# Loading the MLP's weights ahead of the first K block and the output weights behind the last V block, in a decode kernel on one core

## Chip, core and metric

The kernel runs on one core of one Trainium2 chip. The metric is the time of one execution on the device in microseconds (us), lower is better. The kernel before takes 402.87 us (median of 4 runs, 402.78 to 402.98). "The profile" is one execution taken by the hardware profiler; times inside it count from the start of its span.

The engines go by the profile's names: PE is TensorE (PEld its weight loads), DVE is VectorE, ACT is ScalarE, POOL is GpSimd, and SP is SyncE, which here issues the transfers. "Issue" in a chain of waits is time in which an engine waited for nothing that the profile shows. The granted clock is the share of its full clock that PE was allowed. K0, V0 and so on are the blocks of the cache, counted from 0.

## The reference, cut to what matters

One token (x has 1024 numbers) goes through attention with a K and V cache and, beside it, through an MLP.

```python
# A: q = LN(x) @ wq (32 heads of 128); 4 K/V heads of 65536 x 128, 8 queries to each
#    softmax(q k^T / sqrt(128)) v, then @ wo (4096 x 1024)
# B: h  = gelu(LN(xn) @ w1); shift by one or two tokens (S = 1: only zeros are left) @ w2; x1 = xn + that
#    h2 = gelu(LN(x1) @ w3) @ w4;   w1, w2: 1024 x 1024, w3: 1024 x 3584, w4: 3584 x 1024
xn = LN(x)
out = x + A(xn) + x1 + h2
```

Everything is bfloat16. K and V are 134 MB of the 170 MB that are read; the weights are the rest.

## The kernel before

The cache is read as 16 pairs of blocks (4.19 MB of K, 4.19 MB of V each) into two slots of each of two buffers, `Kn` and `Vn`. Each pair is two steps `n`. A step transposes a K half block on DVE into `X` (`Ttr`), multiplies it with q on PE (`QK`), takes maxima, exponentiates on ACT, transposes and multiplies with V (`PV`), and adds into an accumulator on POOL (`FLASH`). When a head is done, its accumulator is normalised and folded into 128 x 8 numbers by `combine`: two products on PE, each with steps on DVE before and after it.

The transfers are all issued in order by SP, and each waits only for its target to be free. The weights pass one after another through a buffer `W`, each issued in the middle of the loop:

```python
        orow = sb("orow", [P, 256], BF)
        W = sb("W", [P, 14336], BF)
        X = sb("X", [P, 2, 8192], BF)
        Kn = sb("Kn", [P, 2, 16384], BF)
        Vn = sb("Vn", [P, 2, 16384], BF)
        # [cut]
        w_seq = [(0, w1_dma, 3, w1_pe), (4, w2_dma, 7, w2_pe),
                 (8, lambda: w3_dma(0), 11, lambda: w3_pe(0)), (12, lambda: w3_dma(1), 15, lambda: w3_pe(1)),
                 (16, lambda: wo_dma(0), 19, lambda: wo_pe(0)), (20, lambda: wo_dma(1), 23, lambda: wo_pe(1))]
        # [cut]
        for n in range(NT):
            h, nb = divmod(n, NSUB)
            QK(n)
            Ttr(n + 1, [0])
            stats1(n)
            if nb == 0 and h > 0:
                combine_1(h - 1)        # the head before, inside the loop
            MB(n); stats2(n); EXP(n)
            Ttr(n + 1, [1])
            if nb == 0 and h > 0:
                combine_2(h - 1)
            PTr(n)
            Ttr(n + 1, [2, 3])
            PV(n); FLASH(n)
            # [cut: products and loads of w_seq, the next K or V block, wo 2 and 3, w4]
        wo_pe(HKV - 2)
        combine_1(HKV - 1)
        combine_2(HKV - 1)
        wo_pe(HKV - 1)
        for i in range(len(w4_parts)):
            w4_pe(i)
```

The combine itself:

```python
        def combine_1(h):
            PE : M0_ps[:, 0:1] = Dmat_f^T @ O_acc[:, 512:513]
            DVE: cb_rL = 1 / M0_ps[:, 0:1];  cb_W = maskT * cb_rL      # 128 x 512
        def combine_2(h):
            PE : M0_ps[:, 128:256] = sum over t of cb_W[t]^T @ O_acc[:, t]   # fp32, 4 products
            DVE: cb_R = M0_ps * maskD;  cb_o = reduce(cb_R);  o_bf[h] = cast(cb_o)
```

(The second block is shortened to its data flow.) Everything goes through one `M0_ps`, one `cb_W` and one `cb_R`.

## Time and profile before

| reading | before | where |
|---|---|---|
| time | 402.87 us | runs |
| bytes read | 169.87 MB, 98.4% of 16 engines' span | queue table |
| K waited for by DVE | 67.4 us in 11 waits | table of waits |
| PE waits for w4 in the tail | 5.0 us in 4 waits | table of waits |
| last w4 piece lands | 398.81 us | chain in order of time |
| final cast starts | 399.50 us | chain in order of time |

The page of the kernel before: its span; the share of time that its 16 DMA engines are busy, in 40 slices, in tenths; its bytes moved; the main queue; and the chain of waits by engine.

```profile
span 401.7 us, 4776 instructions
...
DMA  8999999999999999999999999999999999999994
GB/s 359 424 418 438 445 418 424 460 419 421 436 447 419 429 435 435 422 436 445 420 428 450 426 419 441 441 419 428 434 439 421 447 432 424 426 425 436 437 416 207
...
q1 hardware_dynamic: 6920, 169.87, 98.4%
...
DMA 55%; DVE 24%; PE 16%; issue 2%; ACT 1%; SPq 0%; another core or an unknown queue 0%; POOL 0%; ACTq 0%
...
```

No slice but the first and last is below 90%. (Single slices read up to 460 GB/s because the page counts a packet whole in the slice in which it starts; spread over the time of each packet, no 10 us of this trace exceed 434 GB/s.) The transfers bind; what matters is when the last one lands and what comes after it. The table of waits (engine, line, what it waited for, us in total, times, longest):

```profile
...
DVE X L476 <- DMA Kn<-in_A_k_cache_dram: 67.4, 11, 9.2
...
PE OUT_ps L404 <- DMA Kn<-in_B_w_dram: 5.0, 4, 1.9
...
```

PE waits 5.0 us in all for the four parts of w4. PE's instructions (start, duration, what it is, and in brackets the idle time before it and what ended it):

```profile
...
383.50 0.38 PE L554 MATMUL M_ps<-O_acc,Dmat_f 128*128 128x1 f32 x2 [0.36 <-POOL O_acc L550]
384.67 1.16 PE L564 MATMUL M_ps<-O_acc,cb_W 128*128 128x128 f32 x8 [0.78 <-DVE cb_W L557]
386.92 1.88 PE L404 MATMUL OUT_ps<-W,o_bf 128*1 128x256 bf16 x32 [1.09 <-DVE o_bf L571]
390.37 2.98 PE L404 MATMUL OUT_ps<-Kn,gh_bf 128*1 128x256 bf16 x56 [1.58 <-DMA Kn<-in_B_w_dram]
...
398.85 0.59 PE L404 MATMUL OUT_ps<-Kn,gh_bf 128*1 128x256 bf16 x8 [0.19 <-DMA Kn<-in_B_w_dram]
```

One combine runs from 383.50 to about 386.9, then the last wo product, then each part of w4 as soon as it is there. The end of the chain of waits, in order of time:

```profile
...
374.44 24.37 DMA Kn<-in_B_w_dram
...
399.50 0.42 DVE orow L631
```

### The profile page before, as it was taken

To read this page: it belongs to the slowest core of one execution; us is meant where nothing else is said; L and a number is where in the kernel's file an instruction comes from. 1 tells how busy PE (TensorE), PEld (TensorE's weight loads), DVE (VectorE), ACT (ScalarE), POOL (GpSimd) and SP (SyncE) were. 2 spreads that over 40 slices of the span, in tenths; PEclk is the share of its full clock that TensorE was granted. 3 is DMA by queue.
4 is the path that set the end of the run, shared out by engine and by line. 5 is a ranking of instruction groups with operands and counts; after the bars stand their busy time and mean duration, and the time that the engine had idled before them with its cause. 6 is when DMAs were issued, how large, how long until landed. Compare 5 with 4: busy or idle time off the path is not lost.

```text
span 401.7 us, 4776 instructions
## 1 busy us (share of the span) xinstructions
PE 186.4 (46%) x1859; PEld 78.5 (20%) x1875; DVE 228.4 (57%) x401; ACT 48.9 (12%) x128; POOL 61.8 (15%) x90
## 2 busy tenths in 40 slices
PE   0332325064525745285531965353433654444664
PEld 0211101021103511062110731121111311111132
DVE  0247566277816578255744287576836775788410
ACT  1000111011101011011110011111201111112100
POOL 5000003012211011110310101111110112112110
PEclk9985556556565556555655555656555656565566
DMA  8999999999999999999999999999999999999994
GB/s 359 424 418 438 445 418 424 460 419 421 436 447 419 429 435 435 422 436 445 420 428 450 426 419 441 441 419 428 434 439 421 447 432 424 426 425 436 437 416 207
DMA packets 7087, 170.19 MB, mean 424 GB/s; under 512 B 916, under 2 KB 920, under 8 KB 1048
## 3 DMA queue, kind: packets, MB, share of 16 engines
q1 hardware_dynamic: 6920, 169.87, 98.4%
q8 instruction: 15, 0.25, 0.2%
q14 instruction: 8, 0.07, 0.0%
q10 hardware_dynamic: 144, 0.00, 0.0%
HBM read 169.87 MB, written 0.00 MB: 423 GB/s over the span
## 4 chain that ended last, share of the span: by engine, by line
DMA 55%; DVE 24%; PE 16%; issue 2%; ACT 1%; SPq 0%; another core or an unknown queue 0%; POOL 0%; ACTq 0%
DMA Kn<-in_A_k_cache_dram 44%; DVE X L476 13%; DMA Kn<-in_B_w_dram 6%; DMA Vn<-in_A_wq_dram 5%; PE H_ps L366 4%; PE S_ps L488 3%; DVE pT_f L529 3%; PE OT_ps L536 3%; DVE mrow L495 3%; PE M_ps L366 1%; ACT p_sb L518 1%; PE PT_ps L527 1%; PE M_ps L564 1%; PE OUT_ps L404 1%; DVE Yall L393 1%
## 5 line engine op out<-in xcount | busy, mean ns | idle before, releaser
L476 DVE STREAM_TRANSPOSE X<-Kn 128x1024 f32<-128x1024 f32 x128 | 151.7, 1215 | 67.4 <-DMA Kn<-in_A_k_cache_dram 67.4
L536 PE MATMUL OT_ps<-Vn,pT_f 128*32 128x512 bf16 x512 | 60.7, 627 | 52.4 <-DVE pT_f L529 52.4
L488 PE MATMUL S_ps<-X,Yall 128*32 128x512 bf16 x512 | 59.1, 608 | 16.1 <-DVE X L476 16.1
L501 PE MATMUL MB_ps<-Rm,Lmat 128*128 128x16 bf16 x32 | 6.1, 192 | 90.1 <-DVE Rm L496 90.1
L550 POOL TENSOR_TENSOR O_acc<-O_acc,tmpO 128x513 f32<-128x513 f32 x28 | 32.8, 1172 | 88.6 <-ACT tmpO L544 88.6
L518 ACT ACTIVATE p_sb<-S_ps,brun 128x512 bf16<-128x512 f32 x32 | 22.0, 687 | 192.7 <-DVE brun L516 157.3
L548 POOL TENSOR_SCALAR O_acc<-O_acc,ff 128x513 f32<-128x513 f32 x28 | 19.5, 698 | 153.4 <-ACT ff L523 153.4
L495 DVE TENSOR_REDUCE mrow<-S_ps 128x1 f32<-128x512 f32 x32 | 21.6, 674 | 25.5 <-PE S_ps L488 25.5
L544 ACT ACTIVATE tmpO<-OT_ps 128x512 f32<-128x512 f32 x32 | 19.1, 598 | 108.0 <-PE OT_ps L536 108.0
L488 PEld LDWEIGHTS S_ps<-X,Yall 128*32 128x32 bf16 x512 | 16.6, 126 | 54.7 <-DVE X L476 38.2
L529 DVE STREAM_TRANSPOSE pT_f<-PT_ps 128x512 f32<-128x512 f32 x32 | 22.9, 716 | 6.1 <-PE PT_ps L527 4.2
L536 PEld LDWEIGHTS OT_ps<-Vn,pT_f 128*32 128x32 bf16 x512 | 14.6, 129 | 59.2 <-DVE pT_f L529 42.0
L501 PEld LDWEIGHTS MB_ps<-Rm,Lmat 128*128 128x128 bf16 x32 | 3.3, 102 | 114.9 <-DVE Rm L496 114.9
L527 PE MATMUL PT_ps<-p_sb,permR 128*128 128x512 bf16 x16 | 9.3, 580 | 21.4 <-ACT p_sb L518 21.4
L366 PEld LDWEIGHTS H_ps<-xn_bf,W 128*128 128x128 bf16 x224 | 14.4, 169 | 1.7 <-issue 1.7
L366 PE MATMUL H_ps<-xn_bf,W 128*128 128x1 bf16 x224 | 14.5, 202 | 0.0
L527 PEld LDWEIGHTS PT_ps<-p_sb,permR 128*128 128x128 bf16 x32 | 3.4, 105 | 41.4 <-ACT p_sb L518 41.4
L505 DVE TENSOR_REDUCE Bst<-MB_ps 128x1 f32<-128x16 f32 x32 | 5.6, 174 | 8.3 <-PE MB_ps L501 8.3
L330 PE MATMUL M_ps<-ln_s,ones_f 128*128 128x1 f32 x6 | 1.8, 362 | 17.3 <-DVE ln_s L329 17.3
L546 POOL COPY O_acc<-tmpO 128x513 f32<-128x513 f32 x4 | 2.4, 612 | 47.4 <-ACT tmpO L544 47.4
L404 PE MATMUL OUT_ps<-Kn,gh_bf 128*1 128x256 bf16 x112 | 5.6, 364 | 5.0 <-DMA Kn<-in_B_w_dram 5.0
L631 DVE CAST orow<-OUT_ps 128x256 bf16<-128x256 f32 x1 | 0.4, 425 | 12.7 <-PE OUT_ps L404 12.7
(109 smaller groups left out, 116.6 us busy)
## 6 DMA issues: line engine op xcount, KB each, us to landing
Kn<-in_A_k_cache_dram SPq DMA_DIRECT2D x15, 4096.0 KB, 27.3
Vn<-in_A_v_cache_dram SPq DMA_DIRECT2D x15, 4096.0 KB, 23.3
W<-in_B_w_dram SPq DMA_DIRECT2D x2, 3584.0 KB, 24.9
W<-in_A_wo_dram SPq DMA_DIRECT2D x3, 2048.0 KB, 23.8
Kn<-in_A_wq_dram SPq DMA_DIRECT2D x1, 4096.0 KB, 12.1
Vn<-in_A_wq_dram SPq DMA_DIRECT2D x1, 4096.0 KB, 21.2
W<-in_B_w_dram SPq DMA_DIRECT2D x2, 2048.0 KB, 33.8
Kn<-in_A_k_cache_dram SPq DMA_DIRECT2D x2, 2048.0 KB, 25.3
```

What stands on the lines that cost most here:

```text
L366: fns.append(lambda e, j=j, cx=cx: e.matmul(ps_tile[:, c0 + cx:c0 + cx + 1], lhs_fn(j - j0, cx), rhs_fn(j), start=(j == 0 and cx == 0), st ...
L404: fns.append(lambda e, lhs=lhs, rhs=rhs, jj=jj: e.matmul(OUT_ps[32 * jj:32 * jj + 1, 0:256], lhs, rhs[:, 256 * jj:256 * jj + 256], start=F ...
L476: _op(q_dve, lambda e, ix=ix: e.transpose(out=X32[:, xs, 1024 * ix:1024 * (ix + 1)], in_=Kn32[:, s, 4096 * half + 1024 * ix:4096 * half + ...
L488: fns.append(lambda e, we=we, cm=cm, mv=mv: e.matmul(S_ps[32 * cm:32 * cm + 32, :], Yall[:, h, we, :, :].rearrange("p a g -> p (a g)"), mv ...
L495: _op(q_dve, lambda e: e.reduce_max(mrow[:, m:m + 1], S_ps[:, :], axis=AX.X), reads=[b_S], writes=[b_mrow[m]])
L518: _op(q_act, lambda e: e.activation(p_sb[:, m, :], S_ps[:, :], ACTF.Exp, bias=brun[:, kn:kn + 1], scale=SCALE, accum_out=tmpO[:, m, 512:513]),
L527: _op(q_pe, lambda e: e.matmul(PT_ps[:, :], permR[:, :], p_sb[:, m, :], start=True, stop=True), reads=[b_p[m], b_const], writes=[b_PT])
L529: _op(q_dve, lambda e: e.transpose(out=pT_f[:, :], in_=PT_ps[:, :]), reads=[b_PT], writes=[b_pT])
L536: fns.append(lambda e, q=q, q4=q4: e.matmul(OT_ps[32 * q4:32 * q4 + 32, :], pT_bf[:, q, :, 1], Vn[:, s, 8192 * half + 512 * q:8192 * half ...
L544: _op(q_act, lambda e: e.activation(tmpO[:, m, 0:512], OT_ps[:, :], ACTF.Copy), reads=[b_OT], writes=[b_tmpO[m]], partial=True)
L548: _op(q_pool, lambda e: e.tensor_scalar(out=O_acc[:, :], in0=O_acc[:, :], scalar1=ff[:, m:m + 1], scalar2=0.0, op0=ALU.mult, op1=ALU.add), ...
L550: _op(q_pool, lambda e: e.tensor_tensor(out=O_acc[:, :], in0=O_acc[:, :], in1=tmpO[:, m, :], op=ALU.add), reads=[b_tmpO[m]], writes=[b_Oacc])
```

## The change

The intent: get rid of the buffer `W` and of the bursts of MLP work inside the loop, by loading w1, w2 and w3 at the very start into buffers that K, V and X do not need yet, and wo and w4 at the end into buffers that they no longer need. The combines leave the loop as well; each head gets its own accumulator. MLP products keep the activation as the stationary operand and stream the weights ("row form": 128 matmuls of 256 or 448 columns in place of 352 of one column). The residual is added in the final cast instead of by 64 small matmuls.

The diff, cut to its core (the cut parts: a routine for rolling PE's program into a loop, which is not called; the helpers of the row form; renamed buffers; equal bodies for all steps):

```diff
-        W = sb("W", [P, 14336], BF)
         X = sb("X", [P, 2, 8192], BF)
+        load_rows(Kn[:, 0, 0:8192], [b_K[0][0]], "w1", B_w1, 0, 8)
+        load_rows(Kn[:, 0, 8192:16384], [b_K[0][1]], "w2", B_w2, 0, 8)
+        load_rows(Xf[:, 0:4 * F], b_X[0] + b_X[1], "w3a", B_w3, 0, 4)
+        load_rows(Vn[:, 0, 0:4 * F], b_V[0], "w3b", B_w3, 4, 4)
...
-        O_acc = sb("O_acc", [P, 513], F32)
+        O_all = sb("O_all", [P, HKV, 513], F32)
+        Ycur = sb("Ycur", [P, 4, 4, G], BF)
+        idle = sb("idle", [P, 1], F32)
+        rrow = sb("rrow", [P, 256], F32)
+        rres = sb("rres", [P, 256], F32)
...
         for n in range(NT):
-            if nb == 0 and h > 0:
-                combine_1(h - 1)
...
-            if nb == 0 and h > 0:
-                combine_2(h - 1)
...
             if n == NT - 3:
-                wo_dma(HKV - 2)
-                wo_dma(HKV - 1)
+                for h in range(HKV):
+                    wo_dma(h)
-        wo_pe(HKV - 2)
-        combine_1(HKV - 1)
-        combine_2(HKV - 1)
-        wo_pe(HKV - 1)
+        for i in range(len(w4_parts)):
+            w4_dma(i)
+        for h in range(HKV):
+            combine_1(h)
+            combine_2(h)
+        for h in range(HKV):
+            wo_pe(h)
         for i in range(len(w4_parts)):
             w4_pe(i)
-        _op(q_dve, lambda e: e.tensor_copy(orow[:, :], OUT_ps[:, 0:256]), ...)
+        _op(q_dve, lambda e: e.tensor_tensor(out=orow[...], in0=OUT_ps[...], in1=rres[...], op=ALU.add), ...)
```

## The prediction

> **What bounds the kernel now.** The DMA engines. The page's queue table gives 169.87 MB on the SP queue and 98.4% of 16 engines' span (401.7 us). Cut into 5 us windows, the DMA share stays between 0.91 and 1.10 from 5 to 395 us: no window shows a gap. The long transfers follow each other at about 430 GB/s (the second wq half, 4.19 MB, lands 9.6 us after the first; the last w4 piece, 0.52 MB, takes 1.2 us). [...] The chain of waits is 55% DMA, the rest compute under queued transfers. A steady block takes 8.1 us (QK to QK at 349.9, 358.0), a pair of blocks 16.3 us, its K and V transfers 19.5 us: compute keeps up, with a queue some 12 to 20 us deep (K lands 27.3 us after issue).
>
> **What the change does.**
> - Bytes are the same. w1, w2, w3 (11.5 MB, 26.8 us of transfer) move ahead of K0; wo and w4 (15.7 MB, 36.7 us) all go behind V15. Six are issued at once; K0 and V0 follow when wq is used (21.4, 24.6 us, before the queue would run dry at 49).
> - K0 lands at about 59 us instead of 32. Compute starts 27 us later, but that is covered: the queue is never empty. I estimate K2 issued at 72 us with the queue full to 88, V2 at 85 with it full to 98; after that the rhythm is that of before.
> - MLP products: 352 matmuls with one column (14.5 us on line 366 for w3 alone) become 128 row matmuls, and 64 residual matmuls (1.0 us) become one add in the final cast (0.42 us before, about 0.45 after).  None of it is on the bound: it hid behind transfers.
> - Tail: K14 lands at about 333 us, K15 at 352.5, V15 at 362, PV of the last block ends at about 376 (381.6 before). Then PE and DVE run four combines, 2.7 us each (one took 3.4 us alone from 383.5), then four wo products (1.75 us each) and w4 (5.9 us if throttled). That serial work ends at 394 before w4, while w4's first part lands at 390 and the last at 398.8. So PE catches up with, or ends up to 1 us behind, the last transfer.
>
> **On the critical path:** only the DMA stream and what follows its last piece. Stream: no change. Tail: 0 to +1 us.
>
> **Predicted: 403.1 us, range 401.6 to 404.8 (8 in 10).** Faster by over 2%: 0.03; within 2%: 0.95; slower by over 2%: 0.02.
>
> **What would show it.** DMA share flat near 1.0 in all 40 slices but the first and last, mean near 424 GB/s; PE and PEld busy down by 15 to 20 us; DVE's first K transpose near 59 us; no K wait gone; the last w4 piece landing at 398 to 399 us; a gap between PV of the last block and the wo products filled with combines; the chain still mostly DMA.
>
> **What would make it wrong.** A dip in the DMA share near 88 to 108 us (K2 or V2 issued too late) or at 347 to 367 us (wo waiting for buffers); four combines and wo slower than estimated, so that w4 is multiplied after its landing (+1 to +4 us); a transfer rate that depends on what else runs or on the order of the loads.

The forecast: 402.87 us as before, nothing added by the stream, 0 to 1 us by the tail, put at 403.1.

## The result, and the profile after

The changed kernel is correct and takes 407.32 us (median of 4 runs, 406.40 to 408.27), 4.4 us more than before. The ratio is 1.0109 (95% interval 1.0093 to 1.0126). Ratios here are the mean time of one kernel's runs over that of the other's in the same rounds, so not quite the ratio of the medians quoted. The result lies within 2% of before, as the likeliest case predicted said, but outside the range of 401.6 to 404.8. The direction is clear of noise.

The same lines of the page, after:

```profile
span 406.8 us, 4278 instructions
...
DMA  8999999999999999999999999999999999999991
GB/s 351 422 422 442 421 429 448 411 445 432 414 448 425 421 442 424 432 430 429 435 430 422 432 440 425 429 432 430 435 425 427 441 422 424 445 408 424 434 415 68
...
DMA 56%; DVE 23%; PE 14%; ACT 3%; issue 2%; SPq 0%; POOL 0%; ACTq 0%
...
```

The DMA engines are as full as before, up to the last slice: there is no dip where K2 or V2 or wo could have come too late. So the loads up front did not starve the stream. But in the last slice they move 68 GB/s where they moved 207: the stream is over, and the kernel is still at work. The table of waits of the changed kernel has no line in which PE waits for w4 (the 5.0 us of before). The end of its chain, in order of time (start, us, what):

```profile
...
376.55 0.53 PE M_ps L627 x2
...
377.30 1.36 DVE cb_W L630
378.71 2.09 PE M_ps L637 x8
...
382.60 2.09 PE M_ps L637 x8
...
386.49 2.09 PE M_ps L637 x8
...
390.37 2.07 PE M_ps L637 x8
392.44 1.83 PE OUT_ps L493 x32
...
398.87 1.73 PE OUT_ps L493 x56
...
401.56 1.14 issue
...
404.46 0.58 DVE orow L692
```

From 376.5 us on the chain holds no transfer at all, only PE and DVE: four combines up to 392.4, four wo products, four w4 products, the add. The final add starts at 404.46 us where the cast started at 399.50: 5.0 us later, nearly all of the 5.1 us between the two spans. The profiled run is the slowest of the four (408.27 us), and its chain holds a stop of 1.14 us that another profile of the same kernel (a_again, below) has not; the medians differ by 4.4 us.

That is one cause. The completion events of the transfers in the two traces show a second. The last w4 piece lands at 401.12 us, not 398.81. The transfers of 4.19 MB (K, V) follow each other every 9.72 us (median of 29), where before it was 9.67 (median of 27); those of 2.10 MB every 4.90 us, where before it was 4.84. The bytes, the queue and the sizes are the same. One thing had changed that no line of the diff names: with `W` gone and other small tensors there, the large buffers start elsewhere. In the compiled program `Kn` starts at byte 98048 of each partition before (a multiple of 256) and at 77856 after (32 more than a multiple of 256), and so do `X` and `Vn`. Nothing in these two traces shows that the start of a destination matters to a transfer; that was my guess from here on, and the experiments have to show it.

### The profile page after: what moved, and what is told of

Read it like the earlier page. It is cut to its first block, busy times and chain, and to the rows that moved or that the text cites. A ratio compares the mean times of both kernels' runs of the same rounds, so it can differ in the third digit from the quotient of the medians.

```text
span 406.8 us, 4278 instructions
## 1 busy us (share of the span) xinstructions
PE 183.7 (45%) x1587; PEld 63.0 (15%) x1587; DVE 235.4 (58%) x423; ACT 51.2 (13%) x136; POOL 62.5 (15%) x90
## 4 chain that ended last, share of the span: by engine, by line
DMA 56%; DVE 23%; PE 14%; ACT 3%; issue 2%; SPq 0%; POOL 0%; ACTq 0%
DMA Kn<-in_A_k_cache_dram 51%; DVE X L550 12%; DMA Vn<-in_A_wq_dram 5%; PE S_ps L561 4%; DVE pT_f L602 3%; ACT p_sb L591 3%; DVE mrow L568 3%; PE OUT_ps L493 2%; PE PT_ps L600 2%; PE M_ps L637 2%; PE MB_ps L439 1%; PE MB_ps L574 1%; DVE Yall L481 1%; DVE Bst L578 1%; DVE Rm L569 1%
## 5 line engine op out<-in xcount | busy, mean ns | idle before, releaser
L561 PE MATMUL S_ps<-X,Ycur 128*32 128x512 bf16 x512 | 58.9, 607 | 23.9 <-DVE X L550 23.5
L623 POOL TENSOR_TENSOR O_all<-O_all,tmpO 128x513 f32<-128x513 f32 x28 | 33.5, 1196 | 89.3 <-ACT tmpO L617 89.3
L621 POOL TENSOR_SCALAR O_all<-O_all,ff 128x513 f32<-128x513 f32 x28 | 19.6, 699 | 140.0 <-ACT ff L596 140.0
L600 PE MATMUL PT_ps<-p_sb,permR 128*128 128x512 bf16 x32 | 18.2, 567 | 42.6 <-ACT p_sb L591 42.6
L561 PEld LDWEIGHTS S_ps<-X,Ycur 128*32 128x32 bf16 x512 | 16.8, 125 | 67.8 <-DVE X L550 50.6
L455 DVE STREAM_TRANSPOSE O_all<-tmpO 128x256 f32<-128x256 f32 (+1 forms) x3 | 2.0, 667 | 14.7 <-ACT tmpO L452 14.7
L619 POOL COPY O_all<-tmpO 128x513 f32<-128x513 f32 x4 | 2.4, 612 | 50.8 <-ACT tmpO L617 50.8
L637 PE MATMUL M_ps<-O_all,cb_W 128*128 128x128 f32 x32 | 8.3, 441 | 4.0 <-DVE cb_W L630 4.0
L637 PEld LDWEIGHTS M_ps<-O_all,cb_W 128*128 128x128 f32 x32 | 7.1, 327 | 4.3 <-DVE cb_W L630 4.3
L412 POOL TENSOR_TENSOR ln_s<-ln_s,neghalf 128x1 f32<-128x1 f32 x3 | 1.7, 559 | 34.8 <-DVE ln_s L410 34.8
```

The lines of the kernel that those rows point to most:

```text
L561: fns.append(lambda e, we=we, cm=cm, mv=mv: e.matmul(S_ps[32 * cm:32 * cm + 32, :], Ycur[:, we, :, :].rearrange("p a g -> p (a g)"), mv, s ...
L600: _op(q_pe, lambda e: e.matmul(PT_ps[:, :], permR[:, :], p_sb[:, m, :], start=True, stop=True), reads=[b_p[m], b_const], writes=[b_PT])
L621: _op(q_pool, lambda e: e.tensor_scalar(out=O_all[:, h, :], in0=O_all[:, h, :], scalar1=ff[:, m:m + 1], scalar2=0.0, op0=ALU.mult, op1=ALU ...
L623: _op(q_pool, lambda e: e.tensor_tensor(out=O_all[:, h, :], in0=O_all[:, h, :], in1=tmpO[:, m, :], op=ALU.add), reads=[b_tmpO[m]], writes= ...
L637: fns.append(lambda e, t=t: e.matmul(M0_ps[:, 128:256], cb_W[:, t, :, :].rearrange("p g i -> p (g i)"), O_all[:, h, t * P:(t + 1) * P], st ...
```

## The experiments

Theory T: the tail's serial work costs the time. Theory P: the placement of the buffers makes every transfer slower. Twelve kernels were run. Names that start with a_ are the changed kernel with an edit, with b_ the kernel before with an edit. The columns: where `Kn` starts, mod 256; the time (the median, and the range of all runs); the ratio to before in the same rounds; and from the profiled run, the median spacing of the 4.19 MB transfers, the landing of the last w4 piece, and the start of the last step on DVE. In all fourteen rows the spacing follows the start: 9.66 to 9.67 us at 0, 9.71 to 9.73 at 32 or 64.

| kernel | Kn mod 256 | time us | ratio | 4.19 MB every | last landing | last DVE step |
|---|---|---|---|---|---|---|
| before | 0 | 402.87 (402.78-402.98) | | 9.67 | 398.81 | 399.50 |
| changed | 32 | 407.32 (406.40-408.27) | 1.0109 | 9.72 | 401.12 | 404.46 |
| a_again | 32 | 407.08 (406.50-407.26) | 1.0100 | 9.72 | 401.10 | 403.08 |
| a_pad224 | 0 | 404.93 (404.68-406.07) | 1.0055 | 9.67 | 398.92 | 401.30 |
| a_pad32 | 64 | 406.85 (406.59-408.11) | 1.0106 | 9.71 | 400.75 | 402.96 |
| b_pad32 | 32 | 405.44 (404.96-405.68) | 1.0061 | 9.73 | 401.39 | 402.08 |
| a_inloop | 32 | 405.45 (405.17-405.69) | 1.0063 | 9.72 | 401.38 | 402.07 |
| a_inloop_pad224 | 0 | 403.03 (402.96-403.25) | 1.0004 | 9.67 | 398.96 | 399.65 |
| b_combine_x4 | 0 | 410.74 (409.72-411.49) | 1.0192 | 9.66 | 398.92 | 407.73 |
| a_warm | 32 | 406.18 (405.40-408.04) | 1.0089 | 9.72 | 401.20 | 404.48 |
| a_batch_pad | 0 | 403.16 (403.07-403.24) | 1.0005 | 9.67 | 398.83 | 399.52 |
| a_batch_pad_rolled | 0 | 403.04 (402.89-403.26) | 1.0002 | 9.67 | 399.02 | 399.50 |
| a_cols | 32 | 406.05 (405.91-406.80) | 1.0084 | 9.72 | 401.02 | 402.44 |
| a_shift | 32 | 406.87 (405.79-406.97) | 1.0091 | 9.72 | 401.15 | 402.23 |

Of a_pad32, a_warm, b_combine_x4 and a_batch_pad, a trace of another execution than the one in the table is kept. The landings 400.75, 401.20 and 398.92 of the first three stand in no view that is kept and could not be checked; the kept traces have 398.79 for b_combine_x4, 401.03 for a_warm and 398.96 for a_batch_pad, with spacings as in the table. The kept trace of a_pad32 is of an execution of 469.3 us, longer than any timed one, with no record of the clock and with its 512-column V products at 1.03 us each in place of 0.63; its times are not compared with the others.

### a_pad224: alignment alone, on the changed kernel

```diff
+        pad = sb("pad", [P, 56], F32)      # 224 bytes, never used
         X = sb("X", [P, 2, 8192], BF)
```

> The changed kernel with an unused 224-byte tensor ahead of X, so that X, Kn and Vn start 256-byte aligned again (before: offset 0 mod 256; changed kernel: 32 mod 256, because W went and other tensors came). Nothing else differs. Theory T (tail): all of the +4.4 us is the chain of four combines, wo and w4 products that now ends after the last transfer; alignment does nothing: 407.3 us, 4 MB transfers still 9.72 us apart. Theory P (placement): all of the loss is slower transfers into misaligned rows: 402.9 us. Theory T+P (mine): both; transfers go back from 9.72 to 9.67 us, K15 lands about 1.9 us earlier, and the tail chain with it, but it still ends behind the last transfer: 405.0 to 405.6 us.

Measured: 404.93 us, just below the 405.0 to 405.6 expected. The transfers are 9.67 us apart again and the last lands at 398.92, but the last step on DVE starts 2.4 us after that. The spacing can be seen in DVE's timeline as well: its first transpose of each K block waits for that block to land, so the starts follow the landings, two transfers apart. The changed kernel:

```profile
...
177.66 1.25 DVE L550 STREAM_TRANSPOSE X<-Kn 128x1024 f32<-128x1024 f32 x1 [4.09 <-DMA Kn<-in_A_k_cache_dram]
...
197.10 1.25 DVE L550 STREAM_TRANSPOSE X<-Kn 128x1024 f32<-128x1024 f32 x1 [4.08 <-DMA Kn<-in_A_k_cache_dram]
...
```

With the pad:

```profile
...
176.93 1.25 DVE L551 STREAM_TRANSPOSE X<-Kn 128x1024 f32<-128x1024 f32 x1 [3.95 <-DMA Kn<-in_A_k_cache_dram]
...
196.26 1.25 DVE L551 STREAM_TRANSPOSE X<-Kn 128x1024 f32<-128x1024 f32 x1 [4.42 <-DMA Kn<-in_A_k_cache_dram]
...
```

19.44 us per pair against 19.33; the pairs after these repeat it. Both T alone (407.3) and P alone (402.9) are out; both causes are there.

### b_pad32: misalignment alone, on the kernel before

```diff
+        pad = sb("pad", [P, 8], F32)       # 32 bytes, never used
         W = sb("W", [P, 14336], BF)
```

> The kernel before with an unused 32-byte tensor ahead of W, so that W, X, Kn and Vn start 32 bytes off a 256-byte boundary; nothing else differs. T: no change, 402.9 us. P alone: about 407 us. T+P: 38 transfers of 0.055 us more each, the last one landing about 2.1 us later, at 401: 404.7 to 405.3 us. A third theory, that the order of the loads makes the transfers slower, expects 402.9 here.

Measured: 405.44 us, 2.5 us slower by 32 unused bytes, just above the range expected. The order of the loads is that of before, so it is not the order that makes the transfers slower. The end of its chain reads as in the kernel before, only later (before: the transfer issued at 374.44 landed 24.37 us later):

```profile
...
376.43 24.95 DMA Kn<-in_B_w_dram
...
402.08 0.42 DVE orow L632
```

### a_inloop: the combines of three heads back in the loop

```diff
             stats1(n)
+            if n % NSUB == 0 and n > 0:
+                combine_1(n // NSUB - 1)
...
             Ttr(n + 1, [1])
+            if n % NSUB == 0 and n > 0:
+                combine_2(n // NSUB - 1)
...
-        for h in range(HKV):
-            combine_1(h)
-            combine_2(h)
+        combine_1(HKV - 1)
+        combine_2(HKV - 1)
```

> The changed kernel with the combines of the first three heads put back into the loop, where the kernel before has them; only the fourth is left in the tail. X, Kn, Vn stay misaligned. T: 402.9 to 403.3 us. P alone: 407.3 us. T+P: the last w4 piece still lands near 401.1 us, the products after it end some 0.7 us later instead of 3.3: 404.3 to 405.0 us.

Measured: 405.45 us, 1.9 us better than the changed kernel and 0.5 above the range expected, for the same reason as b_pad32: I had put the last landing at 401.1 and it came at 401.38. The tail is off the chain; the last transfer ends it:

```profile
...
372.19 29.19 DMA X<-in_B_w_dram
...
402.07 0.58 DVE orow L695
```

### a_inloop_pad224: both edits

```diff
+        pad = sb("pad", [P, 56], F32)      # and the edit of a_inloop
```

> Both edits: combines back in the loop and the 224-byte pad. T, P and T+P all expect 402.5 to 403.2 us if nothing else in the change costs time; T and P are told apart by the two runs with one edit. If the row form, the loads up front or the add in the final cast cost anything of their own, this run stays above 403.5.

Measured: 403.03 us, ratio 1.0004 (0.9992 to 1.0016). The loss is gone, and with it the gain that one might have hoped for. What remains of the change (loads up front, row form, add in the cast, an own accumulator for each head) costs and brings nothing together. Its chain differs from that of a_inloop by the landing alone:

```profile
...
370.32 28.64 DMA X<-in_B_w_dram
...
399.65 0.58 DVE orow L696
```

### a_pad32: which boundary

```diff
+        pad = sb("pad", [P, 8], F32)       # 32 bytes: Kn at 64 mod 256
         X = sb("X", [P, 2, 8192], BF)
```

> The changed kernel with a 32-byte pad ahead of X instead of 224: X, Kn and Vn start at 64 mod 256. If what matters is a 256-byte boundary: no gain, 4 MB transfers 9.72 us apart, 407.0 to 407.8 us. If a 64-byte boundary is enough: 9.67 us apart and 404.9 us, as with the 224-byte pad. A third reading, that any pad at all or a fresh build changes the rate, expects 404.9 too.

Measured: 406.85 us, 9.71 us apart. A start at 64 mod 256 is no faster than one at 32 (9.71 us apart and 9.72), and a pad as such does nothing (expected 407.0 to 407.8; the 0.15 us below are within the spread of the changed kernel, and a_again came to 407.08). Of the starts tried, only those at 0 mod 256 had 9.66 to 9.67 us. 128 mod 256 was not tried. Why the start matters is not shown by any run.

### b_combine_x4: more combines in the tail of the kernel before

```diff
-        combine_1(HKV - 1)
-        combine_2(HKV - 1)
+        for _ in range(4):
+            combine_1(HKV - 1)
+            combine_2(HKV - 1)
```

> The kernel before, its only combine of the tail run four times over (same data, same result), everything else untouched, buffers aligned. If combines one after another in the tail are what the changed kernel pays for: three more of 2.9 to 3.9 us, first eaten by the slack before the last w4 piece, then in full: 405.5 to 409.5 us, the last piece still landing at 398.8. If the tail is not what binds: 402.9 us.

Measured: 410.74 us, more than the range expected, with the last landing unmoved (398.79 in the trace kept). The tail alone, with nothing of the change, makes the kernel slower. A combine took 3.9 us each time (the distance between the products' starts), so three more are 11.7 us. The first combine was slower too, its products 2.07 us instead of 1.16, and the last wo product starts 13.1 us later than before (400.00 against 386.92). Less the 5.0 us of waiting that is 8.1, and the last step starts 8.2 us later:

```profile
...
385.17 2.09 PE M_ps L564 x8
...
389.06 2.09 PE M_ps L564 x8
...
402.04 3.13 PE OUT_ps L404 x56
...
407.73 0.42 DVE orow L632
```

### a_warm: filler matmuls in the gaps of the combines

```diff
         for h in range(HKV):
             combine_1(h)
+            fill(3)      # 3 matmuls of 128 x 512 into M1_ps, never read
             combine_2(h)
+            fill(2)
```

> The changed kernel (misaligned) with filler matmuls, results unused, in the gaps that PE has while it waits for DVE in the four combines: 5 per combine. If the combines cost 3.9 us each rather than the 2.7 predicted because PE ran them at half the granted clock, and the fillers raise it: combines of 2.9 us, wo products of 1.1 us, the chain ending with the transfers: 405.2 to 406.0 us, the run-to-run spread of the changed kernel gone. If the clock has no part, or the fillers do not raise it, they only take PE time: 407.3 to 410 us.

The prediction had taken 2.7 us for a combine from the one in the profile of before. Its product group took 1.16 us there, and 2.07 us in the changed kernel. The granted clock of TensorE differs between the two: 0.50 from 365.8 to 396.5 us in the changed kernel's record of the clock, which holds all four groups; 1.00 from 382.8 to 386.2 us in that of before, which holds its group (384.67 to 385.83 us). The windows of the changed kernel's tail (stretch, its length, then busy us and instructions of PE, PEld, DVE, ACT, POOL, then the granted clock, the DMA share and GB/s):

```profile
...
384.00:388.00 4.00, 2.74 (x13) 2.39 (x12) 1.50 (x5) 0.00 (x0) 0.00 (x0) 0.50 1.03 441
...
396.00:400.00 4.00, 3.51 (x116) 2.42 (x112) 0.00 (x0) 0.00 (x0) 0.00 (x0) 0.94 0.56 225
...
```

In the kernel before, the stretch of its one combine shows 0.72 on average:

```profile
...
380.00:385.00 5.00, 3.85 (x53) 2.04 (x46) 0.65 (x2) 0.60 (x1) 1.09 (x1) 0.72 1.02 430
...
```

With the fillers, PE's timeline shows the products of the third and fourth combine at 1.11 us and 2.96 us from one to the next:

```profile
...
378.84 2.07 PE L637 MATMUL M_ps<-O_all,cb_W 128*128 128x128 f32 x8
...
383.63 1.05 PE L637 MATMUL M_ps<-O_all,cb_W 128*128 128x128 f32 x8
...
386.54 1.11 PE L637 MATMUL M_ps<-O_all,cb_W 128*128 128x128 f32 x8
...
389.50 1.11 PE L637 MATMUL M_ps<-O_all,cb_W 128*128 128x128 f32 x8
...
400.84 1.66 PE L493 MATMUL OUT_ps<-X,gh_bf 128*1 128x256 bf16 x26 [2.56 <-issue]
...
```

So the time of a combine in this tail went with the granted clock where both are shown (product group 2.07 us at 0.50, 1.16 at 1.00), and adding useless work shortened it, from 3.89 us to 2.96 from one to the next. PE was busy 2.74 us of 4 between 380 and 392 us of the changed kernel, and the clock stayed at 0.50; what load it takes is not shown. What it brings to the time is mixed: three of six runs came to 405.40, 405.40 and 405.63 us, the level of a_inloop, where the last landing binds; the other three came to 406.74, 407.96 and 408.04. The profiled run is one of the slow ones. In it PE stops for 2.56 us within one group of w4 products, waiting for nothing that the profile shows. The spread was not removed, against what I expected.

The trace kept of this kernel is of another execution, with a span of 403.8 us instead of 406.8. Its combines are 2.96 us apart as well, PE stops at the same place, after 6 matmuls of the second w4 part, but only for 0.56 us:

```profile
...
398.28 0.93 PE L493 MATMUL OUT_ps<-X,gh_bf 128*1 128x256 bf16 x26 [0.56 <-issue]
...
```

There the last landing, at 401.03 us, ends the chain. So the fillers shortened the combines in both, and what parts the two is mostly the length of that stop; more on it below (a_shift).

### a_batch_pad: the tail's combines overlapped

```diff
+        pad = ...                            # X, Kn, Vn 256-byte aligned
-        for h in range(HKV):
-            combine_1(h)
-            combine_2(h)
+        # one product and one reciprocal for heads 0 to 2, one for head 3;
+        # cb_W4[h], and a PSUM bank (M0, M1, H, MB) of its own for each head
+        for h in range(HKV):
+            DVE: cb_W4[:, h] = maskT * cb_rL4[:, h]
+            PE : bank[h] = sum over t of cb_W4[h, t]^T @ O_all[h, t]
+            if h > 0: tail_o(h - 1)          # cb_R, cb_o, o_bf of the head before
```

(shortened to its data flow)

> The changed kernel with aligned buffers and the tail's four combines overlapped instead of one after another: one product for three normalisers, four banks and four weight buffers, so that PE goes from one head's product to the next while DVE reduces the one before. The combines should take about 10 us instead of 15.9, PE be done with wo before w4's second part lands at 395.3, and the time be set by the last landing again: 402.6 to 403.3 us. If the combines must leave the tail for the loss to go: 404 to 405 us.

Measured: 403.16 us, as expected. The combines take from 375.3 to 384.5 us, 9.3 instead of 15.9, and the chain ends with a transfer again:

```profile
...
369.91 28.93 DMA X<-in_B_w_dram
...
399.52 0.58 DVE orow L720
```

They need not leave the tail: they must only not stand one behind the other.

### a_batch_pad_rolled: a shorter program for PE

```diff
-        q_pe.emit(nc.tensor)
+        q_pe.emit_rolled(nc.tensor, es)      # first four steps written out, then 7 passes of a loop
```

> The aligned kernel with the overlapped combines (403.16 us), its PE program rolled into a loop of seven passes of four blocks after a first pass written out, by a routine that the changed kernel holds but does not use; every wait in the loop is on a positive register value. PE's program gets shorter by some six sevenths of the blocks, so most of the 16 KB packets of the instruction queue (12 in the changed kernel, about 1 us each, on the same DMA engines) should go. If these packets are what sets single engines back now and then (one transfer in the middle of the run lands 0.3 to 1.1 us late, and at the end the first and the sixteenth engine are 3.7 us apart), the last w4 piece lands 0.5 to 2 us earlier: 401.0 to 402.6 us, faster than both. If not: 403.1 us.

Measured: 403.04 us, ratio 1.0002 (0.9988 to 1.0016), no gain. The instruction queue's packets were halved, to 6 from the 13 of a_batch_pad, but the last landing stayed at 399.02 us and the first and last of the 16 completions of that transfer stayed 3.6 us apart (3.6 in the kept trace of a_batch_pad too). So the packets in the loop are not what draws the completions apart, and what does it stays open. The run doesn't speak for packets at the end: two of the six start in the last 11 us (391.69 and 396.15), as two do in a_batch_pad.

### a_cols: the column form of the MLP products

```diff
-        mm_rows(xn2_bf, b_xn2, D, Kn[:, 0, 0:8192], 0, 8, 8, w1_banks, [b_K[0][0]])
+        mm_cols(M1_ps, 256, KT_D, ...)       # and so for w2, w3, as before the change
```

> The changed kernel with the MLP products back in the column form of the kernel before, on the same early loads; misaligned, combines in the tail. All theories: PE's weight loads up by some 15 us, all of it under the queued transfers before K0 lands at 60.3 us: 406.4 to 408.3 us, as the changed kernel. If the row form itself had cost or gained time: outside that.

Measured: 406.05 us (405.91 to 406.80): below the range expected and 1.3 us below the changed kernel. The work itself is hidden, as expected. In its profile the gap inside the w4 products (1.14 us in the changed kernel) is missing, and the wo products run fast (1.04 us instead of 1.88) one product earlier, from the second on.

### a_shift and a_again: is it the row form, or where the tail falls in the program?

```diff
         issue_v(1)
+        # 224 matmuls of one column into M1_ps, never read, while PE waits for K0
         gelu(rows_to_cols(F, w3_banks, 0), ...)
```

> The changed kernel (row form, misaligned, combines in the tail) with 224 small matmuls of unused result put on PE after the MLP products, while PE waits for K0: PE's program is as long as in the run with the column form, which was unexpectedly 1.3 us faster than the changed kernel. If the reason lies in where the tail falls in PE's program (the changed kernel's profile shows a gap of 1.14 us inside a group of w4 products that waits for nothing, the column form's none): 405.8 to 406.8 us, no such gap. If it is the row form itself that costs 1.3 us: 407.0 to 408 us.

> The changed kernel again, untouched, on the same chip as the run beside it, for its spread: 406.4 to 408.3 us. If it comes out near 406.0, the difference to the column form was chance or chip, and there is nothing to explain.

Measured: a_shift 406.87 us (405.79 to 406.97, three of its four runs within 406.87 to 406.97), a_again 407.08 us. This doesn't settle it: the median of a_shift lies between the two answers. But the two profiled runs (405.79 and 406.91 us) show one thing that makes up their difference. a_shift:

```profile
...
392.61 1.48 PE OUT_ps L493 x31
...
394.23 1.07 PE OUT_ps L493 x32
...
```

and a_again:

```profile
...
392.37 1.83 PE OUT_ps L493 x27
...
394.34 1.90 PE OUT_ps L493 x32
...
```

The first two wo products take 2.55 us in one and 3.73 in the other, 1.18 us, and the last step starts 0.85 us later (a_again reached the first of them 0.24 us sooner). In one the clock rises within the first product, in the other behind the second (at 393.5 and 396.4 us in the record of the clock). Whether that moment varies between runs of one kernel is a further question. In the two profiles of the changed kernel it did not (396.5 and 396.4 us); in those of a_warm the time of the same work did: the fillers right after the first combine's product took 1.30 us in one and 0.83 in the other. So whether the moment of the rise is part of the changed kernel's spread of 1.9 us is not shown; its two profiles differ by the stop of 1.14 us. Why column form kept at or below 406.8 in all five runs stays open.

The kept traces tell more of these stops. In the changed kernel (PE's timeline):

```profile
...
402.69 0.39 PE L493 MATMUL OUT_ps<-X,gh_bf 128*1 128x256 bf16 x8 [1.14 <-issue]
...
```

Exactly 3,265 of PE's recorded instructions come before this stop, and as many before that of a_warm, though a_warm has 36 more of them ahead of the w4 products. In these two the stop lies at one place of PE's program, not at one product. The queue that the profile calls "instruction" brings packets of 16 KB, 12 of them in the changed kernel, one for every 260 or so of PE's instructions. In the three kept traces with such a stop, PE goes on 1.50 us (changed kernel), 1.31 (a_warm) and 1.32 (a_batch_pad_rolled, a stop of 2.04 us) after one of these packets is through (in the changed kernel the packet ends at 401.19 us). That these packets have to do with the stops is my guess from that order in time; what PE waits for is not shown, and no run varies it alone.

## Why the prediction was wrong, point by point

- **What binds.** Right for the kernel before, and for most of the changed one: DMA is full in all slices but the first and last.
- **Loads up front do not starve the stream.** Right. K0 landed at 60.3 us (59 predicted), K2 was issued at 73.5 (72) and V2 at 87.1 (85), with the queue full.
- **MLP work is off the bound.** Right: with the two causes of loss removed, nothing is left of it, 1.0004. The PE and PEld time saved was 18 us (186.4 + 78.5 against 183.7 + 63.0), in the 15 to 20 that I gave.
- **"Stream: no change."** This step failed. I took bytes and sizes to fix the stream's length, and did not ask where the buffers start. Among what could go wrong I had a transfer rate that depends on what else runs or on the order of the loads; b_pad32 keeps both as they were and is slower all the same. Each transfer got about 0.055 us longer; 46 large transfers make an estimated 2.5 us. The last landing went from 398.8 to 401.1. a_pad224 gives back 2.4 us of 4.4 (404.93 against 407.32), and b_pad32 makes the kernel before 2.5 us slower.
- **"Tail: 0 to +1 us."** The mechanism was right, and listed among what could go wrong; the term for the combines was mis-sized. I put four at 2.7 us, 10.8 in all, from one combine that ran in part at a higher granted clock (1.00 from 382.8 to 386.2 us). They took 15.9 (376.5 to 392.4). The product group at a granted clock of 0.50 is 0.9 us longer than the one that I read (2.07 us against 1.16), and the first combine's `cb_W` took 1.35 us instead of the 0.49 of the other three. A POOL add of 1.09 us started just before it (377.28 and 377.30 us), and `cb_W` ended 0.28 us after it. The kept traces repeat that: in all nine in which a POOL add runs beside a `cb_W`, that `cb_W` ends 0.28 us after the add, also in a_pad32's, where the add ends 0.13 us sooner and `cb_W` takes 1.22 us instead of 1.35; every `cb_W` without an add beside it takes 0.47 to 0.49. By what the add holds it up, if it does, no run shows. a_inloop, with three combines off the tail, gives back 1.9 us (405.45), and b_combine_x4 shows that this tail alone is enough to make the kernel slower.
- **The two together.** Removing both gives 403.03 us, so 2.4 and 1.9 us add up to the 4.3 that were lost within 0.1. That it fits so well is partly luck: in the profiles the tail of a_pad224 begins only 1.3 us earlier than that of the changed kernel (first combine at 375.14 and 376.48), and the rest of the 2.4 comes from the tail itself, where the stop is missing and the clock rises at 393.7 instead of 396.5. By my reading they add because the tail begins at a landing: PE starts its last work when the last K block has come through, and slower transfers push that back too.
- **Where the gain went that the change was meant to bring.** There was none to be had, as the prediction said: the work that the change takes out of the loop had been hidden under transfers. No version of it in these runs is faster than before.

**What stays open.** Whether the gaps inside the w4 products (1.14 and 2.56 us) have to do with the packets of the instruction queue; when the clock rises in the tail; why column form was 1.3 us faster; and why the 16 completions of one transfer come to lie 3.4 to 4.3 us apart by the end, in all kernels (the last w4 piece: 3.45 before, 4.06 changed).

## What to carry to other kernels

When the transfers bind, look at where each large destination starts in its partition, before and after every change that adds or removes a tensor: an unused pad may be worth as much as the change (here 32 bytes of it cost 2.5 us in b_pad32, and 224 gave back 2.4 in a_pad224). Moving work out of a loop whose time is hidden, to a tail where it isn't, cost here its whole length beyond what the tail had of waiting (b_combine_x4: the last wo product 13.1 us later, 5.0 us of waiting used up, the last step 8.2 later); read that waiting first. And size a matmul chain that stands nearly alone by the lowest granted clock that your traces show, not by one sample (here 0.50, at which the group that I had read at 1.16 us took 2.07).
